# One core, three stages: the first product of the second block by column blocks of its weights over all tokens, with the weights converted there

## Chip, core and metric

The kernel runs on one core of one Trainium2 chip. The metric is the device time of one execution in microseconds (us). Engines: TensorE (PE, matmuls; PEld its weight loads), VectorE (DVE), ScalarE (ACT), GpSimd (POOL), SyncE (SP, which issues most DMAs). Each engine works through its own instructions in their order.

## What is computed

Clustered attention, a mixture of experts, and a dense second block, one after the other, in float64 inputs that carry float32 precision. What matters here:

```python
def _moe_ref(x, w_gate, w_output_gate, w1, w2):        # x: 1536 x 512, 8 experts
    ...
    for e in range(E):
        mask = e_idx == e
        ...
        h = np.maximum(x[mask] @ w1[e], 0.0)           # 512 -> 1024
        ye = h @ w2[e]                                 # 1024 -> 512
        out[mask] = gate_w[mask, None] * eom[mask, e, None] * ye

def _moe2_ref(x, w_in, w_out):                         # 512 -> 2048 -> 512
    h = x @ w_in
    ...
    g = np.where(pos, h, np.where(neg, 0.0, (h + beta) ** 2 / (4.0 * beta)))
    return (g @ w_out).astype(np.float32)
```

## The kernel before

Every matmul operand is held as two float16 halves, high and low, and a product is three matmuls: high x high, high x low, low x high. So each weight has to be split on the chip after its transfer: ScalarE scales and rounds it to the high half, and VectorE (L1012) or GpSimd (L1009, after an extra ScalarE pass L1007) subtracts to get the low half.

**Experts.** The experts run in order of their size, with room for CAPS = 304, 256, 224, 208, 192, 176, 176, 144 tokens. Their weights come in pieces of 512 KB, four for w1 and four for w2 of each expert, through a ring of six buffers (`stg`). Round r has twelve steps: four units of the second product of expert r (`l2`, 24 matmuls each) and eight of the first product of expert r + 1 (`l1`, 12 matmuls each). In each step first the next piece is asked for on SP's queue (w2 of r + 1, then w1 of r + 2), then the unit's matmuls are issued, and then `pipe.step()` issues what earlier steps left behind for it: the split of a piece one step later on ScalarE and one more step later on VectorE or GpSimd, the evacuation of a unit one step later (`hT`, the hidden halves, by ScalarE L1094 and VectorE L1095; `y`, the product times its gate, by VectorE L1111, then its two halves into `x2` by ScalarE L1113 and VectorE L1114). A round ends with a gate matmul (L1074). Units take their PSUM from a ring of seven banks. The tokens of an expert come by a transposing DMA from `xs`, into which the routing has scattered them (L646).

**w_in.** The weights of the second block are 64-bit words. `piece64` loads 512 KB (128 columns of w_in) into a ring of three buffers; one step later VectorE puts the float32 together in three operations (`cw`, L1032 to L1034, in one PSUM bank); one step later ScalarE makes the high half and a float32 copy; one step later GpSimd subtracts (L1041). NWI = (2, 2, 1, 1, 1, 0, 0, 0) blocks stand at the end of the piece list of each round; the other nine follow in the second block.

**Second block.** The 1536 tokens are three groups of 512. `m1(g, fc)` makes one block of 128 hidden columns for one group: 12 matmuls of 512 columns into one of six banks, then two VectorE, two ScalarE and one GpSimd operation (L1242 to L1250). All 16 blocks of group 0 come first, with nine w_in and five w_out conversions between them, then the second product of group 0 with the other eleven w_out blocks, then the first product of groups 1 and 2, then their second products. The engines take a branch (L1190) between the experts and the second block.

Of the kernel before, what the change touches and what calls it, by code (L numbers as in the profile page):

```python
# [140 lines left out]
def build(tc, q, k, v, centroids, w_gate, w_og, w1, w2, w_in, w_out, out):  # L141
# [842 lines left out]

    big = root.enter_context(tc.tile_pool(name="big", bufs=1))
    x2 = big.tile([128, 2, KD, NTK + CMAX], F16, name="x2")
    wih = big.tile([128, KD, F2], F16, name="wih")
    wil = big.tile([128, KD, F2], F16, name="wil")
    st6 = root.enter_context(tc.tile_pool(name="st6", bufs=3))
    cv = root.enter_context(tc.tile_pool(name="cv", bufs=2))  # L990
    mes = ExitStack()
# [22 lines left out]
    def piece(dst_h, dst_l, src, scale):  # L1014

        a, b = dst_h.shape[1], dst_h.shape[2]
        t = stg.tile([128, a, b], F32, tag="st", name="stg")
        n_lo[0] += 1
        nc.sync.dma_start(out=t, in_=src)
        pool = n_lo[0] > 4 and n_lo[0] % 8 in (1, 4, 6)  # L1020
        pipe.add(lag[0], lambda: halves(dst_h, dst_l, t, scale, pool))

    def piece64(dst_h, dst_l, src, scale):

        a, b = dst_h.shape[1], dst_h.shape[2]
# [3 lines left out]
        def words():
            hi, lo = t[:, :, :, 1], t[:, :, :, 0]  # L1030
            c = psc[0].tile([128, a, b], I32, tag="c", name="cw")
            nc.vector.tensor_scalar(out=c, in0=hi, scalar1=5, scalar2=2, op0=ALU.logical_shift_left, op1=ALU.logical_shift_right)  # L1032
            nc.vector.scalar_tensor_tensor(out=c, in0=hi, scalar=-2 ** 30, in1=c, op0=ALU.bitwise_and, op1=ALU.bitwise_or)  # L1033
            nc.vector.scalar_tensor_tensor(out=c, in0=lo, scalar=29, in1=c, op0=ALU.logical_shift_right, op1=ALU.bitwise_or)  # L1034
            f = c.bitcast(F32)

            def split():
                x = cv.tile([128, a, b], F32, tag="cv", name="cv")
                nc.scalar.activation(out=dst_h, in_=f, func=AF.Copy, scale=scale)
                nc.scalar.activation(out=x, in_=f, func=AF.Copy, scale=scale)  # L1040
                pipe.add(1, lambda: nc.gpsimd.tensor_tensor(out=dst_l, in0=x, in1=dst_h, op=ALU.subtract))  # L1041
            pipe.add(1, split)
        pipe.add(1, words)
# [53 lines left out]
    def l2(r, dc):  # L1097
        cap, c0 = CAP[r], C0[r]
        wh, wl = W[r, 2]
        p = ps.tile([128, 512], F32, tag="p", name="yps")  # L1100
        d = slice(dc * 128, (dc + 1) * 128)
        h = HT[r]
        for f in range(KF):
            nc.tensor.matmul(out=p[:, 0:cap], lhsT=wh[:, f, d], rhs=h[:, 0, f, :], start=(f == 0), stop=False)  # L1104
            nc.tensor.matmul(out=p[:, 0:cap], lhsT=wh[:, f, d], rhs=h[:, 1, f, :], start=False, stop=False)  # L1105
            nc.tensor.matmul(out=p[:, 0:cap], lhsT=wl[:, f, d], rhs=h[:, 0, f, :], start=False, stop=(f == KF - 1))  # L1106
        g = G[r]

        def scaled():
            y = yp.tile([128, cap], F32, tag="y", name="y")  # L1110
            nc.vector.tensor_tensor(out=y, in0=p[:, 0:cap], in1=g, op=ALU.mult)  # L1111
            y0, y1 = x2[:, 0, dc, ds(c0, cap)], x2[:, 1, dc, ds(c0, cap)]
            pipe.add(1, lambda: nc.scalar.activation(out=y0, in_=y, func=AF.Copy))  # L1113
            pipe.add(2, lambda: nc.vector.tensor_tensor(out=y1, in0=y, in1=y0, op=ALU.subtract))  # L1114
        pipe.add(1, scaled, True)
# [2 lines left out]
    ACTDVE = [ET.Activation, ET.DVE]  # L1118
    eid = {}

    NWI = (2, 2, 1, 1, 1, 0, 0, 0)

    def expert(r):
        if r < E:
            eid[r] = reg(regs[0:1, 0, r:r + 1], [ET.SP], E - 1)

    wi2 = w_in.bitcast(I32)
    wiq = [lambda f=f: piece64(wih[:, :, f * 128:(f + 1) * 128], wil[:, :, f * 128:(f + 1) * 128],
                               wi2[:, f * 256:(f + 1) * 256].rearrange("(k p) (f z) -> p k f z", p=128, z=2), SWI) for f in range(KF2)]
# [20 lines left out]
    for r in range(E):  # L1150
        expert(r + 2)
        C0[r] = reg(regs[0:1, 2, r:r + 1], ACTDVE, NTK)
        ld_q = (w2_pieces(r + 1, eid[r + 1]) if r + 1 < E else []) + (w1_pieces(r + 2, eid[r + 2]) if r + 2 < E else [])
        ld_q += [wiq.pop(0) for _ in range(NWI[r])]
        a, b = 0, 0
        if r + 1 == E:
            pipe.flush()
            for _ in wnd:
                pass
            nw = nc.values_load(nwin[0:1, 0:1], min_val=0, max_val=NWIN, skip_runtime_bounds_check_because="a count of windows")  # L1160
        if 0 in PAT.get(r, ()):
# [28 lines left out]
    with tc.If(nw > 0):  # L1190
        with tc.For_i(0, nw, 1) as i:
# [12 lines left out]
            for n in range(KD):  # L1204
# [5 lines left out]

    bes = ExitStack()
    wo_p = bes.enter_context(tc.tile_pool(name="wo", bufs=1))
    woh = wo_p.tile([128, KF2, DM], F16, name="woh")
    wol = wo_p.tile([128, KF2, DM], F16, name="wol")
    gp = bes.enter_context(tc.tile_pool(name="gp", bufs=2))
    ep = bes.enter_context(tc.tile_pool(name="ep", bufs=2))
    psc[0] = bes.enter_context(tc.tile_pool(name="psc2", bufs=2, space=PSUM))
    ps2 = bes.enter_context(tc.tile_pool(name="ps2", bufs=6, space=PSUM))
    wo2 = w_out.bitcast(I32)
    woq = [lambda n=n: piece64(woh[:, n:n + 1, :], wol[:, n:n + 1, :],  # L1220
                               wo2[n * 128:(n + 1) * 128, :].rearrange("(k p) (d z) -> p k d z", p=128, z=2), SWO) for n in range(KF2)]
# [64 lines left out]
    for f in range(KF2):
        if woq:
            woq.pop(0)()
        m2_part(0, range(NW), acc, [f])
        pipe.step()  # L1290
    for t in range(NW):
        pipe.add(1 + t // 2, lambda t=t: put(0, t, acc[t]))
    for g in (1, 2):
        for fc in range(KF2):
            m1(g, fc)
            pipe.step()
    for g in (1, 2):
        for t in range(NW):
            p = m2_tile()
# [37 lines left out]
```

## Time and profile before

| | |
|---|---|
| median of 3 runs | 700.89 us (698.8 to 706.71) |
| the profiled execution: time, span | 703.17 us, 701.4 us |
| mean granted TensorE clock | 0.928 of 2.4 GHz |
| attention and routing, to the first expert matmul | 275.25 us |
| first product of expert 0 | 14.60 us |
| rounds 0 to 6 | 24.96, 22.58, 22.34, 17.32, 21.74, 19.81, 14.40 us |
| round 7 and the branch | 8.65 us |
| second block, to the end of the span | 259.75 us |
| busy over the span | PE 605.7, PEld 387.1, DVE 452.4, ACT 388.9, POOL 335.5 us |

Times in the rows are us from the start of the span, durations us unless ns is written. The granted clock is a share of 2.4 GHz; its lower level is 1.2 GHz (0.5). DMA is the mean busy share of the 16 DMA engines. Matmuls overlap, so the distance of their starts is their pace. A waiting instruction is shown with the idle time of its engine and what ended it, as [1.04 <-ACT hT L1094].

### The profile page before, as it was taken

The page shows a single profiled execution, that of the slowest core. Times are in us where ns is not written, and L with a number is a line of the kernel's source. Part 1 is how long each engine was busy: PE and PEld are TensorE (multiplying, and loading weights), DVE is VectorE, ACT ScalarE, POOL GpSimd, SP SyncE. Part 2 cuts the span into 40 slices and gives each one's busy share as a digit, 9 for nine tenths or more (in the row PEclk, how much of TensorE's full clock was granted, in tenths as well). Part 3 has the DMA queues.
Part 4 walks back from the last instruction along what each step waited for, and adds up shares of the span by engine and source line. Part 5 has one row for each costly group of instructions (what it writes and reads, how often), then busy time and mean ns, then how long its engine had stood idle before and what let it go on. Part 6 is the DMA issues. An engine that isn't in the chain of part 4 may idle for free. (4 is left out here: it accounts for less than half of the span.)

```text
span 701.4 us, 14212 instructions
## 1 busy us (share of the span) xinstructions
PE 605.7 (86%) x5574; PEld 387.1 (55%) x5574; DVE 452.4 (64%) x874; ACT 388.9 (55%) x612; POOL 335.5 (48%) x281
## 2 busy tenths in 40 slices
PE   1898679797979753998897999898999999999996
PEld 1365536565656551688797889343444444444442
DVE  6897968898797952687796686599953445500000
ACT  5388558786768911877686785367533444410000
POOL 8368456766476831246465342276634444321101
PEclk9999867798799955999999899999999999999999
DMA  8786998539723429997999994154631000000000
GB/s 212 167 168 148 188 209 214 133 73 159 139 77 84 77 60 271 315 335 159 263 292 204 289 263 142 62 154 143 196 108 60 1 1 0 1 16 30 16 31 30
DMA packets 142171, 96.29 MB, mean 137 GB/s; under 512 B 97168, under 2 KB 127888, under 8 KB 142096
## 3 DMA queue, kind: packets, MB, share of 16 engines
q1 hardware_dynamic: 139744, 88.60, 51.3%
q0 software_dynamic: 2352, 6.70, 2.7%
q8 instruction: 47, 0.77, 0.5%
q14 instruction: 28, 0.23, 0.1%
HBM read 59.84 MB, written 12.29 MB: 103 GB/s over the span
## 5 line engine op out<-in xcount | busy, mean ns | idle before, releaser
L486 POOL TENSOR_TENSOR pl<-p,ph 128x768 f16<-128x768 f32 x64 | 112.8, 1780 | 54.4 <-ACT ph L480 41.2
L445 DVE TENSOR_REDUCE mq<-s 128x1 f32<-128x768 f32 x96 | 90.4, 949 | 23.2 <-PE s L440 23.0
L475 ACT ACTIVATE p<-st 128x768 f32<-128x768 f32 x96 | 75.9, 810 | 38.6 <-PE st L471 35.6
L1250 POOL TENSOR_TENSOR gt<-gx,gt 128x512 f16<-128x512 f32 x48 | 55.4, 1159 | 72.6 <-ACT gt L1249 72.5
L480 ACT ACTIVATE ph<-p 128x768 f16<-128x768 f32 x96 | 77.5, 847 | 0.8
L508 PE MATMUL pv<-vh,pl 128*128 128x65 f16 x576 | 68.7, 203 | 10.1 <-DVE pl L486 10.1
L1235 PE MATMUL mps<-x,wih 128*128 128x512 f16 x192 | 73.5, 383 | 2.9 <-PEq L1190 2.9
L1244 ACT ACTIVATE sq<-cl,c 128x512 f32<-128x512 f32 x48 | 34.6, 721 | 72.7 <-DVE cl L1242 72.7
L1260 PE MATMUL ops<-woh,gt 128*128 128x512 f16 x192 | 72.8, 379 | 1.5 <-DVE gx L1248 1.5
L1237 PE MATMUL mps<-x,wil 128*128 128x512 f16 x192 | 73.5, 383 | 0.0
L1236 PE MATMUL mps<-x,wih 128*128 128x512 f16 x192 | 73.4, 382 | 0.0
L1261 PE MATMUL ops<-wol,gt 128*128 128x512 f16 x192 | 72.8, 379 | 0.5 <-POOL wol L1041 0.4
L1262 PE MATMUL ops<-woh,gt 128*128 128x512 f16 x192 | 72.8, 379 | 0.0
L470 PE MATMUL st<-aT 128*128 128x384 f16 x192 | 68.4, 356 | 4.4 <-DVE mq L445 3.2
L1242 DVE TENSOR_SCALAR cl<-mps 128x512 f32<-128x512 f32 x48 | 33.1, 689 | 59.8 <-PE mps L1237 59.8
L506 PE MATMUL pv<-vh,ph 128*128 128x65 f16 x576 | 69.6, 204 | 0.0
L507 PE MATMUL pv<-vl,ph 128*128 128x64 f16 x576 | 69.2, 202 | 0.0
L471 PE MATMUL st<-q2T,bT 82*128 82x384 f16 x192 | 68.4, 356 | 0.8 <-DMA q2T<-kq 0.8
L1105 PE MATMUL yps<-hT,w2h 128*128 128x176 f16 (+6 forms) x256 | 63.8, 256 | 6.0 <-DVE hT L1095 5.9
L1104 PE MATMUL yps<-hT,w2h 128*128 128x176 f16 (+6 forms) x256 | 63.6, 255 | 5.4 <-ACT hT L1094 4.1
L1088 PE MATMUL hps<-xt,w1h 128*128 128x176 f16 (+6 forms) x256 | 54.4, 265 | 15.4 <-DMA xt<-xs 14.2
L1106 PE MATMUL yps<-hT,w2l 128*128 128x176 f16 (+6 forms) x256 | 63.9, 256 | 0.0
(220 smaller groups left out, 1483.1 us busy)
## 6 DMA issues: line engine op xcount, KB each, us to landing
stg<-in_moe_w_dram SPq DMA_DIRECT2D x64, 512.0 KB, 7.0
stg<-in_moe_w_in_dram SPq DMA_DIRECT2D x16, 512.0 KB, 6.3
stg<-in_moe_w_out_dram SPq DMA_DIRECT2D x16, 512.0 KB, 3.6
xs<-zrow SPq DMA_DIRECT2D x16, 288.0 KB, 4.0
kqf<-in_k_dram SPq DMA_DIRECT2D x16, 192.0 KB, 3.5
kqf<-in_q_dram SPq DMA_DIRECT2D x16, 192.0 KB, 3.2
vf<-in_v_dram SPq DMA_DIRECT2D x16, 192.0 KB, 3.5
xs<-zrow SPq DMA_DIRECT2D x8, 108.0 KB, 2.9
```

Source lines behind the costliest of these rows:

```text
L445: nc.vector.tensor_reduce(out=mq[:, i, t:t + 1], in_=lg_t.pop((i, t))[:, :, 0:HS], axis=AX.XY, op=ALU.max)
L475: nc.scalar.activation(out=p.rearrange("p (e s) -> p e s", e=2), in_=lg_t.pop(("t", i, c))[:, :, 0:HS], func=AF.Exp, scale=SCALE)
L480: nc.scalar.activation(out=ph_t[i, c], in_=p_t[i, c], func=AF.Copy)
L486: eng.tensor_tensor(out=pl_t[i, c], in0=p_t.pop((i, c)), in1=ph_t[i, c], op=ALU.subtract)
L506: nc.tensor.matmul(out=x[:, 0:D + 1], lhsT=ph[:, sl], rhs=a[:, c, 0:D + 1], start=False, stop=False)
L507: nc.tensor.matmul(out=x[:, 0:D], lhsT=ph[:, sl], rhs=b[:, c, :], start=False, stop=False)
L1235: nc.tensor.matmul(out=p, lhsT=wih[:, kk, f], rhs=x2[:, 0, kk, c], start=(kk == 0), stop=False)
L1236: nc.tensor.matmul(out=p, lhsT=wih[:, kk, f], rhs=x2[:, 1, kk, c], start=False, stop=False)
L1237: nc.tensor.matmul(out=p, lhsT=wil[:, kk, f], rhs=x2[:, 0, kk, c], start=False, stop=(kk == KD - 1))
L1260: nc.tensor.matmul(out=p, lhsT=gt[:, 0, f, c], rhs=woh[:, f, :], start=(f == 0), stop=False)
L1261: nc.tensor.matmul(out=p, lhsT=gt[:, 0, f, c], rhs=wol[:, f, :], start=False, stop=False)
L1262: nc.tensor.matmul(out=p, lhsT=gt[:, 1, f, c], rhs=woh[:, f, :], start=False, stop=(f == KF2 - 1))
```

## The change

1. The second block's first product runs over column blocks: for each of the 16 blocks `fc`, the three groups one after the other. w_in is no longer held whole (`wih`, `wil`) but in a ring of four blocks (`wi_p`); the hidden halves of all three groups are held (`gp` has three buffers).
2. `piece64` is parted into `fetch64` (the load) and `words64` (the conversion). One list orders all 32 blocks; each `convert()` takes the oldest loaded block and asks for the next, so three are under way. The rounds of the experts hold no w_in, but for three loads at the end of round 6's list and three conversions in steps 2, 5 and 8 of round 7. In the second block 21 of the 48 steps of the first product convert a block (13 of w_in, 8 of w_out), and the first eight steps of the second product the rest.
3. `y` is no longer a tile in SBUF: the product is scaled in place in its PSUM bank, and both halves are made from there.
4. Of the expert pieces those with a number of 1 or 5 modulo 8 go to GpSimd, before 1, 4 or 6.
5. As `wih` and `wil` are gone, the tiles of the experts lie at other addresses: `stg` at bytes 72,928 to 97,504 of a partition, before 97,504 to 122,080. Tiles of the routing (`gs`, 72,960 to 79,616) lay there before.

```diff
-    wih = big.tile([128, KD, F2], F16, name="wih")
-    wil = big.tile([128, KD, F2], F16, name="wil")
+    wi_p = root.enter_context(tc.tile_pool(name="wi", bufs=4))
...
-        pool = n_lo[0] > 4 and n_lo[0] % 8 in (1, 4, 6)
+        pool = n_lo[0] > 4 and n_lo[0] % 8 in (1, 5)
...
-            y = yp.tile([128, cap], F32, tag="y", name="y")
-            nc.vector.tensor_tensor(out=y, in0=p[:, 0:cap], in1=g, op=ALU.mult)
+            y = p[:, 0:cap]
+            nc.vector.tensor_tensor(out=y, in0=y, in1=g, op=ALU.mult)
...
-    NWI = (2, 2, 1, 1, 1, 0, 0, 0)
...
+    for fc in range(KF2):
+        if fc + 3 < KF2:
+            slots64[fc, 0] = ("i", fc + 3)
+    nwo = 0
+    for fc in range(KF2):
+        for g in range(3):
+            if (g == 1 and fc % 3 == 1) or (g == 0 and (fc, 0) not in slots64):
+                slots64[fc, g] = ("o", nwo)
+                nwo += 1
...
+    def convert():
+        z, f, t = got.pop(0)
+        if z == "i":
+            WI[f] = [wi_p.tile([128, KD, 128], F16, tag=n, name=n) for n in ("wih", "wil")]
+            words64(t, WI[f][0], WI[f][1], SWI)
+        else:
+            words64(t, WO[0][:, f:f + 1, :], WO[1][:, f:f + 1, :], SWO)
+        fetch()
...
-        ld_q += [wiq.pop(0) for _ in range(NWI[r])]
+        if r + 2 == E:
+            ld_q += [fetch, fetch, fetch]
+        if r + 1 == E:
+            ld_q += [lambda: None] * 2 + [convert, lambda: None, lambda: None] * 3
...
-    gp = bes.enter_context(tc.tile_pool(name="gp", bufs=2))
+    gp = bes.enter_context(tc.tile_pool(name="gp", bufs=3))
...
     for fc in range(KF2):
-        m1(0, fc)
-        if wiq:
-            wiq.pop(0)()
-        elif fc >= KF2 - AHEAD:
-            woq.pop(0)()
-        pipe.step()
+        for g in range(3):
+            m1(g, fc)
+            if (fc, g) in slots64:
+                convert()
+            pipe.step()
     acc = [m2_tile() for _ in range(NW)]
     for f in range(KF2):
-        if woq:
-            woq.pop(0)()
+        if got:
+            convert()
...
-    for g in (1, 2):
-        for fc in range(KF2):
-            m1(g, fc)
-            pipe.step()
```

On VectorE, the end of round 3 (`hT` 128x192 is expert 4's hidden half, x_5482 is `x2`), before:

```order
L1095 SCALAR_TENSOR_TENSOR hT<-hps,hT 128x192
L1114 ISA
L1114 TENSOR_TENSOR x_5482<-y,x_5482 128x208
L1012 SCALAR_TENSOR_TENSOR w1l<-stg,w1h 128x4x256
L1111 TENSOR_TENSOR y<-yps,g 128x208
L1032 TENSOR_SCALAR cw<-stg 128x512
L1033 SCALAR_TENSOR_TENSOR cw<-stg,cw 128x512
L1034 SCALAR_TENSOR_TENSOR cw<-stg,cw 128x512
L1095 SCALAR_TENSOR_TENSOR hT<-hps,hT 128x192 x2
```

and with the change:

```order
L1095 SCALAR_TENSOR_TENSOR hT<-hps,hT 128x192
L1114 ISA
L1114 TENSOR_TENSOR x_5482<-yps,x_5482 128x208
L1011 SCALAR_TENSOR_TENSOR w1l<-stg,w1h 128x4x256
L1111 TENSOR_TENSOR yps<-yps,g 128x208
L1011 SCALAR_TENSOR_TENSOR w1l<-stg,w1h 128x4x256
L1095 SCALAR_TENSOR_TENSOR hT<-hps,hT 128x192 x2
```

The three cw operations ahead of the last two hT of the round are gone; the split of the eighth piece, on GpSimd before, stands in their place.

On SP, the first loads of the experts, with the semaphores that each waits for (DMASW are those of GpSimd's transfers, here the scatters into `xs`; DMAHW those of SP's own), before:

```order
L1046 TENSOR_LOAD regs
L1019 ISA
L1019 DMA stg<-in_moe_w_dram 128x4x256 [waits DMAHW2_49,DMAHW3_49,DMAHW1_49,DMAHW4_49,DMAHW0_49,DMAHW5_49,DVE_49,DMAHW6_49,PE_49,DMAHW7_49,Activation_49,Pool_49]
L1019 ISA
L1019 DMA stg<-in_moe_w_dram 128x4x256 [waits DMAHW4_49]
L1046 TENSOR_LOAD regs
L1065 ISA
L1065 DMA_TRANSPOSE xt<-xs 128x4x304 [waits DMASW7_49,DMAHW5_49,DMASW3_49,DVE_49]
```

and with the change (the row of the first load is cut at its end as printed):

```order
L1046 TENSOR_LOAD regs
L1018 ISA
L1018 DMA stg<-in_moe_w_dram 128x4x256 [waits DMASW6_49,DMASW7_49,DMASW5_49,DMAHW0_49,DMASW4_49,DMAHW1_49,DMASW3_49,DMAHW2_49,DMASW2_49,DMAHW3_49,DMASW1_49,DMAHW4_49,DMASW0_49,DMAHW5_49,DVE_49,DMAHW6_49,PE_49,DMAHW7_49,Activation_49,Poo
L1018 ISA
L1018 DMA stg<-in_moe_w_dram 128x4x256
L1046 TENSOR_LOAD regs
L1065 ISA
L1065 DMA_TRANSPOSE xt<-xs 128x4x304
```

The waits for the scatters have moved from the first transposing load to the first weight load, which stands ahead of it.

## Rows read from the trace of the kernel before

**Rows 1.** Windows, rounds 1 to 6, later products: PE, PEld, DVE, ACT, POOL, PEclk, DMA, GB/s.
```profile
314.81:337.39 22.58, 20.48 (x194) 18.58 (x193) 17.15 (x33) 15.32 (x26) 13.20 (x9) 1.00 0.82 203
337.39:359.73 22.34, 19.97 (x194) 18.84 (x194) 19.74 (x40) 16.39 (x28) 13.48 (x9) 0.92 1.06 269
359.73:377.05 17.32, 17.10 (x195) 16.52 (x194) 13.31 (x27) 13.91 (x25) 12.43 (x8) 1.00 0.98 212
377.05:398.79 21.74, 17.82 (x194) 16.81 (x194) 11.93 (x22) 13.60 (x24) 6.73 (x5) 0.92 1.07 253
398.79:418.60 19.81, 17.22 (x194) 16.16 (x194) 15.76 (x26) 17.34 (x32) 9.71 (x5) 0.91 0.98 283
418.60:433.00 14.40, 13.70 (x194) 13.36 (x193) 11.75 (x25) 10.16 (x23) 4.70 (x3) 1.00 0.68 221
...
537.60:622.50 84.90, 84.90 (x395) 38.48 (x394) 38.35 (x60) 36.74 (x60) 35.41 (x31) 1.00 0.02 8
```

**Rows 2.** Waits of PE, 290 to 434 us: in total, times, longest.
```profile
PE yps L1105 <- DVE hT L1095: 5.9, 7, 2.2
PE yps L1104 <- ACT hT L1094: 4.1, 6, 1.0
PE hps L1088 <- DVE hT L1095: 1.2, 2, 0.9
PE yps L1104 <- DVE y L1111: 1.1, 2, 0.7
PE hps L1089 <- POOL w1l L1009: 0.5, 1, 0.5
```

**Rows 3.** Timeline, PE at 294 us; DVE and PE at 381 us: start, duration.
```profile
294.17 0.29 PE L1104 MATMUL yps<-hT,w2h 128*128 128x304 f16 x1 [1.04 <-ACT hT L1094]
...
381.67 0.69 DVE L1032 TENSOR_SCALAR cw<-stg 128x512 int32<-128x512 int32 x1 [2.11 <-DMA stg<-in_moe_w_in_dram]
...
383.73 0.35 DVE L1095 SCALAR_TENSOR_TENSOR hT<-hps,hT 128x192 f16<-128x192 f32 x1
384.13 0.24 PE L1105 MATMUL yps<-hT,w2h 128*128 128x192 f16 x1 [2.17 <-DVE hT L1095]
```

**Rows 4.** Timeline around the first loads of the experts.
```profile
266.46 0.97 POOL L646 DMA_INDIRECT xs<-pay,pos  x1 [0.30 <-issue]
...
267.16 1.02 SPq L1019 DMA_DIRECT2D stg<-in_moe_w_dram  x2
270.67 1.39 SPq L1065 DMA_TRANSPOSE xt<-xs  x1
...
273.33 2.36 DVE L1012 SCALAR_TENSOR_TENSOR w1l<-stg,w1h 128x1024 f16<-128x1024 f32 x2 [6.11 <-DMA stg<-in_moe_w_dram]
...
275.46 0.46 PE L1089 MATMUL hps<-xt,w1l 128*128 128x304 f16 x1
```

**Rows 5.** VectorE groups by line, 290 to 434 us: busy us, mean ns, idle before.
```profile
L1012 DVE SCALAR_TENSOR_TENSOR w2l<-stg,w2h 128x1024 f16<-128x1024 f32 x23 | 32.0, 1393 | 0.3 <-ACT w2h L1011 0.3
...
L1095 DVE SCALAR_TENSOR_TENSOR hT<-hps,hT 128x176 f16<-128x176 f32 x16 | 5.4, 335 | 10.4 <-ACT hT L1094 10.4
...
L1033 DVE SCALAR_TENSOR_TENSOR cw<-stg,cw 128x512 int32<-128x512 int32 x7 | 4.9, 696 | 0.2
...
L1114 DVE TENSOR_TENSOR x<-y,x 128x176 f32 x7 | 3.0, 433 | 0.0
```

**Rows 6.** Waits of PE in the second block, 441 to 701 us.
```profile
PE mps L1235 <- PEq L1190: 2.9, 1, 2.9
PE ops L1260 <- DVE gx L1248: 1.5, 1, 1.5
PE ops L1261 <- POOL wol L1041: 0.4, 1, 0.4
```

**Rows 7.** The chain that ended last: VectorE, two blocks with a conversion each.
```profile
452.59 0.68 DVE cl L1242
...
455.84 0.68 DVE cl L1242
```

More of the change, by code (lines that the diff above doesn't have):

```diff
@@ L1019, in piece, with fetch64 @@
         nc.sync.dma_start(out=t, in_=src)
-        pool = n_lo[0] > 4 and n_lo[0] % 8 in (1, 4, 6)
+        pool = n_lo[0] > 4 and n_lo[0] % 8 in (1, 5)
         pipe.add(lag[0], lambda: halves(dst_h, dst_l, t, scale, pool))
-    def piece64(dst_h, dst_l, src, scale):
-        a, b = dst_h.shape[1], dst_h.shape[2]
+    def fetch64(src, a, b):
         t = st6.tile([128, a, b, 2], I32, tag="st", name="stg")
         nc.sync.dma_start(out=t, in_=src)
[L1029 to L1043, printed above, removed]
@@ new lines, in fetch64, with words64, split @@
+        return t
+    def words64(t, dst_h, dst_l, scale):
+        a, b = dst_h.shape[1], dst_h.shape[2]
+        hi, lo = t[:, :, :, 1], t[:, :, :, 0]
+        c = psc[0].tile([128, a, b], I32, tag="c", name="cw")
+        nc.vector.tensor_scalar(out=c, in0=hi, scalar1=5, scalar2=2, op0=ALU.logical_shift_left, op1=ALU.logical_shift_right)
+        nc.vector.scalar_tensor_tensor(out=c, in0=hi, scalar=-2 ** 30, in1=c, op0=ALU.bitwise_and, op1=ALU.bitwise_or)
+        nc.vector.scalar_tensor_tensor(out=c, in0=lo, scalar=29, in1=c, op0=ALU.logical_shift_right, op1=ALU.bitwise_or)
+        f = c.bitcast(F32)
+        def split():
+            x = cv.tile([128, a, b], F32, tag="cv", name="cv")
+            nc.scalar.activation(out=dst_h, in_=f, func=AF.Copy, scale=scale)
+            nc.scalar.activation(out=x, in_=f, func=AF.Copy, scale=scale)
+            pipe.add(1, lambda: nc.gpsimd.tensor_tensor(out=dst_l, in0=x, in1=dst_h, op=ALU.subtract))
+        pipe.add(1, split)
@@ L1125, in expert, with fetch @@
             eid[r] = reg(regs[0:1, 0, r:r + 1], [ET.SP], E - 1)
-    wi2 = w_in.bitcast(I32)
-    wiq = [lambda f=f: piece64(wih[:, :, f * 128:(f + 1) * 128], wil[:, :, f * 128:(f + 1) * 128],
-                               wi2[:, f * 256:(f + 1) * 256].rearrange("(k p) (f z) -> p k f z", p=128, z=2), SWI) for f in range(KF2)]
+    wi2, wo2 = w_in.bitcast(I32), w_out.bitcast(I32)
+    WI, WO, got, order64 = {}, {}, [], []
+    for f in range(3):
+        order64.append(("i", f))
+    slots64 = {}
+    for fc in range(KF2):
[7 more added lines that the diff above has]
+                nwo += 1
+    order64 += [slots64[k] for k in sorted(slots64)] + [("o", f) for f in range(nwo, KF2)]
+    feed = list(order64)
+    def fetch():
+        if feed:
+            z, f = feed.pop(0)
+            got.append((z, f, fetch64(wi2[:, f * 256:(f + 1) * 256].rearrange("(k p) (f z) -> p k f z", p=128, z=2), KD, 128) if z == "i" else
+                        fetch64(wo2[f * 128:(f + 1) * 128, :].rearrange("(k p) (d z) -> p k d z", p=128, z=2), 1, DM)))
+    def convert():
[6 more added lines that the diff above has]
+        fetch()
     def row(r):
@@ L1212, in build @@
     wo_p = bes.enter_context(tc.tile_pool(name="wo", bufs=1))
-    woh = wo_p.tile([128, KF2, DM], F16, name="woh")
-    wol = wo_p.tile([128, KF2, DM], F16, name="wol")
-    gp = bes.enter_context(tc.tile_pool(name="gp", bufs=2))
+    WO[0] = woh = wo_p.tile([128, KF2, DM], F16, name="woh")
+    WO[1] = wol = wo_p.tile([128, KF2, DM], F16, name="wol")
+    gp = bes.enter_context(tc.tile_pool(name="gp", bufs=3))
     ep = bes.enter_context(tc.tile_pool(name="ep", bufs=2))
@@ L1218, in build @@
     ps2 = bes.enter_context(tc.tile_pool(name="ps2", bufs=6, space=PSUM))
-    wo2 = w_out.bitcast(I32)
-    woq = [lambda n=n: piece64(woh[:, n:n + 1, :], wol[:, n:n + 1, :],
-                               wo2[n * 128:(n + 1) * 128, :].rearrange("(k p) (d z) -> p k d z", p=128, z=2), SWO) for n in range(KF2)]
     c1 = cst.tile([128, 1], F32, name="c1")
@@ L1231, in m1 @@
         p = ps2.tile([128, N], F32, tag="p", name="mps")
-        f = slice(fc * 128, (fc + 1) * 128)
+        wih, wil = WI[fc]
         c = slice(g * N, (g + 1) * N)
         for kk in range(KD):
-            nc.tensor.matmul(out=p, lhsT=wih[:, kk, f], rhs=x2[:, 0, kk, c], start=(kk == 0), stop=False)
-            nc.tensor.matmul(out=p, lhsT=wih[:, kk, f], rhs=x2[:, 1, kk, c], start=False, stop=False)
-            nc.tensor.matmul(out=p, lhsT=wil[:, kk, f], rhs=x2[:, 0, kk, c], start=False, stop=(kk == KD - 1))
+            nc.tensor.matmul(out=p, lhsT=wih[:, kk, :], rhs=x2[:, 0, kk, c], start=(kk == 0), stop=False)
+            nc.tensor.matmul(out=p, lhsT=wih[:, kk, :], rhs=x2[:, 1, kk, c], start=False, stop=False)
+            nc.tensor.matmul(out=p, lhsT=wil[:, kk, :], rhs=x2[:, 0, kk, c], start=False, stop=(kk == KD - 1))
         g0, g1 = GT[g][:, 0, fc, :], GT[g][:, 1, fc, :]
@@ L1276, in build @@
     NW = N // 128
-    AHEAD = 5
     for fc in range(KF2):
-        m1(0, fc)
-        if wiq:
-            wiq.pop(0)()
-        elif fc >= KF2 - AHEAD:
-            woq.pop(0)()
-        pipe.step()
+        for g in range(3):
[3 more added lines that the diff above has]
+            pipe.step()
     acc = [m2_tile() for _ in range(NW)]
     for f in range(KF2):
-        if woq:
-            woq.pop(0)()
+        if got:
+            convert()
         m2_part(0, range(NW), acc, [f])
```

## The prediction

> **What bounds the kernel now.** I read the windows first, cut at the gate matmuls L1074 that end each round of the experts. Rounds 1 to 6 take 118.2 us together (22.58 + 22.34 + 17.32 + 21.74 + 19.81 + 14.40) [rows 1]. The reader should see that these lengths don't follow the arithmetic. A round streams 96 x (cap of r + cap of r+1) columns: 46,080, 41,472, 38,400, 35,328, 33,792 and 30,720. Round 3, the best of them, takes 17.32 / 38,400 = 0.451 ns a column, and the second block's 395 matmuls of 512 columns 84.90 us, 0.420 ns, both at a granted clock of 1.00. Narrow matmuls won't quite reach the second pace; I use the middle, 0.436. The six rounds, 225,792 columns, would need 98.4 us at it, so about 19.8 us of them are not matmul time. The worst rounds (2, 4, 5) also show a granted clock of 0.92, 0.92 and 0.91: a part of each ran at the lower level, 1.2 GHz.
>
> The waits of the matrix engine say where the rest goes: 12.8 us between 290 and 434 us, 11.2 of them for hT, the hidden halves that ScalarE and VectorE make out of PSUM [rows 2]. They come in bursts at the ends of rounds, and the timeline of the burst at 381 us shows why: VectorE stands 2.11 us for a block of w_in to land, then runs the three cw steps, and only then the hT that is behind them in its order; the matmul waits 2.17 us for that hT [rows 3]. The clock falls right after such a burst. The second block is different: after the last expert the matrix engine waits 1.5 + 0.4 us in all for data [rows 6], and its matrix engine is busy for all of the 84.90 us [rows 1]. So what can be won lies in the rounds, and hardly behind them.
>
> **Term 1, w_in leaves the rounds.** Seven blocks (2, 2, 1, 1, 1 in rounds 0 to 4) lose there a transfer of 512 KB, three cw steps (0.696 us each [rows 5], 2.09 the three), two ScalarE copies and a GpSimd subtraction. Three come back as bare transfers in round 6 and are converted in round 7. Of the 12.8 us of rows 2, 1.1 are for y, and 1.04 stand at 294 us, before the first block is asked for [rows 3]; 10.7 us remain. Clock: 22.34 x 0.08 + 21.74 x 0.08 + 19.81 x 0.09 = 5.3 us [rows 1]. So 16.0 us can be laid to w_in. I take 13.5: late expert weights have a share in it too (0.5 us for w1l [rows 2]), and the eighth piece of each round is now split on VectorE (term 3) where the cw steps stood. Bounds: 5.9 us, if only the waits for VectorE's hT go and no clock comes back, and 19.8 us, the whole excess.
>
> **Term 2, the start of the experts.** The buffers of the weights now lie where tiles of the routing lay, and the order shows it: the first weight load waits for the scatters into xs, for which in the kernel before only the transposing loads wait. The last scatter is issued at 266.46 us, the first load at 267.16, the first transposing load at 270.67 [rows 4]. So the first load moves by up to 3.5 us. Its low half is ready at about 274.5 (the first of two splits that take 2.36 us from 273.33) and used at 275.46 by L1089 [rows 4], a slack of 1.0 us: +2.5 us. Bounds: +1.0, if the load lands faster without the scatters beside it and only the transposing load behind two issues (1.02 us) is late; +4.5, if they slow each other by 2 us. Behind the waiting load on SP's queue stand those transposing loads and all further weights, so nothing hides this.
>
> **Term 3, seven subtractions go from GpSimd to VectorE** (of 64 pieces 15 stay on GpSimd, before 22). VectorE gets one more split a round, 1.39 us [rows 5], and loses cw; ScalarE loses one extra pass. In rounds 3 to 5 VectorE was busy 13.31, 11.93 and 15.76 us [rows 1]: mean 13.7, less 2.1 for a cw trio, plus 1.4, is 13.0 us against 15.6 us of matmuls (107,520 columns at 0.436 ns, by three). Covered: 0; if round 5 stays as full as it was, its 15.76 us against 14.7, +1 to +2.
>
> **Term 4, y stays in PSUM.** No instruction is added. VectorE reading PSUM costs no more here than reading SBUF: hT at 176 columns 335 ns out of PSUM, x at 176 columns 433 ns out of SBUF [rows 5]. What it does cost is the bank: it comes free with y's last reader, two units of work later than with its first. With seven banks the matrix engine may lead VectorE by four units instead of six. It already waited 1.1 us twice for y [rows 2]. I take +1.0; bounds 0 and one wait of a unit (14.7 / 12 = 1.23 us) in each of rounds 3 to 6, +4.9.
> The Trainium skill speaks against this edit: "VectorE: DVE Perf Modes" (section on the TRN2 errata) gives VectorE 120 fixed cycles for a PSUM source and 58 for an SBUF one, 65 ns more at its 0.96 GHz. By it 32 reads of y would cost 2.1 us of VectorE, and were all of that on the path, the sum below would be 691.1 and not 689.0. Rows 5 don't show that difference, and I go by the rows.
>
> **Term 5, round 7 and the hand-over.** Three trios of cw, six copies and three subtractions stand now among the last y and x. One trio stands ahead of the last two writes of x2. The matrix engine waits 2.9 us for its branch there in any case [rows 6], and the first product reads the fourth column block of x2 only after nine matmuls. So 0; without that cover +2.0, the trio.
>
> **Term 6, second block.** A block of the first product without a conversion takes VectorE 1.28 us (38.35 us for 60 instructions, two a block) and the matrix engine 2.58 us (12 x 84.90 / 395) [rows 1]. All 48 blocks and 21 conversions are 48 x 1.28 + 21 x 2.09 = 105 us of VectorE in 124 us of matmuls; the densest group, three blocks and two conversions, is 8.0 against 7.7, the next ones 5.9 against 7.7. Before, 16 blocks carried 14 conversions, 3.25 us each [rows 7] against 2.58, and VectorE fell behind until the second product waited 1.9 us. That wait goes, since two more blocks now lie between the last block of group 0 and the second product: -1.9 (bound 0). Transfers run three conversions ahead, 3 x 124 / 21 = 18 us. The tail is the same.
>
> **Sum.** -13.5 + 2.5 + 0 + 1.0 + 0 - 1.9 = -11.9 us. The profiled execution has a span of 701.4 in a time of 703.17 us, 2.3 us above the median of 700.89. So its span goes to 689.5, and against the median I predict **689.0 us**.
>
> **Rivals.**
> - *The transfers go on to set the pace.* For: the shares of 0.98 to 1.07 in rounds 2 to 5, at 256 GB/s over them (time-weighted) [rows 1]. Then a round shrinks by its bytes alone: the five blocks of rounds 1 to 4, 2.62 MB, are 10.2 us; with the other terms -8.6, **692.3 us**. Against: shares of 0.82 in round 1 and 0.68 in round 6.
> - *The whole excess goes*, as every burst fed the next: -19.8 + 2.5 - 1.9 = -19.2, **681.7 us**. For: clock and lateness carry over from round to round. Against: one more split a round on VectorE.
> - *Slower: the banks.* If VectorE lags by four units, 4.9 us, in the narrow rounds, each of the 16 second products of rounds 3 to 6 holds the matrix engine up by a unit, 16 x 1.23 = 20 us: 689.0 - 1.0 + 20 = **708 us**. For: the y waits are waits for a bank, at the old limit of six units. Against: two of them in 144 us, 1.1 us in all, and less work ahead of y in both queues.
> - *It only moves the work*: conversions that hold the second block up as they did the rounds. For this VectorE would need 19 us more there (105 against 124), and I see nothing that gives it; 3 in 100, at about **700 us**.
>
> **How the numbers follow.** Forecast (684 to 694) 0.56, transfers 0.20, whole excess 0.12, banks 0.07, moved only 0.03, a worse start or hand-over 0.02. A change under 1% (7 us) is about what a measurement of this kernel can't tell from none. Faster by over 1%, below 693.9: most of the forecast (0.54), the whole excess and a quarter to a third of the transfers: 0.72. Within 1%: 0.20. Slower: 0.08. The range leaves out the slow rival and the ends of the others: 682 to 697.
>
> **What would show it.** Term 1: no hT wait over 1 us at the ends of rounds 1 to 4, a granted clock near 1.00 in rounds 2, 4 and 5, rounds 1 to 6 in about 105 us. Term 2: the first load at 270 us or later, the first L1089 near 278. Term 4: waits of yps or hps matmuls for the x subtraction L1114; over 5 us of them and the banks decide. Term 6: no wait of ops for gx, VectorE no busier than 0.9 in the first product. Rounds 2 to 5 still at shares of 1 and near 18 us each would be the transfers. Wrong altogether: rounds 1 to 6 above 112 us, or holes among the mps matmuls.

## The result and the profile after

The changed kernel takes 694.68 us in the median of four runs (694.36 to 694.92), the kernel before 699.89 us beside it. The ratio is 0.988, with a 95% interval of 0.983 to 0.993, and 0.985 (0.980 to 0.990) when it ran a second time on another chip: faster by 1.2 to 1.5%. The ratio is taken over undisturbed executions and isn't the quotient of the two medians (0.993): the kernel before ranges from 698.8 to 706.7 us here, and the verdicts below go by ratios. By the ratio the gain is 8 to 11 us. The forecast was 689.0 us with a range of 682 to 697. The profiled execution has a span of 692.6 us against 701.4, that is -8.8 where the sum of the terms said -11.9.

The windows of rounds 1 to 6, cut at the gate matmuls as in [rows 1] (columns: PE, PEld, DVE, ACT, POOL, granted clock, DMA share, GB/s):

```profile
318.62:338.62 20.00, 20.00 (x195) 18.61 (x194) 15.42 (x31) 13.77 (x23) 9.38 (x6) 1.00 1.00 216
338.62:356.68 18.06, 18.06 (x195) 17.77 (x194) 10.51 (x25) 11.76 (x19) 9.70 (x6) 1.00 1.05 239
356.68:375.19 18.51, 16.99 (x195) 16.60 (x194) 14.94 (x30) 14.04 (x25) 9.58 (x6) 1.00 1.04 238
375.19:390.68 15.49, 15.49 (x195) 15.24 (x194) 11.93 (x20) 11.84 (x21) 5.36 (x3) 1.00 1.05 291
390.68:407.59 16.91, 15.06 (x195) 14.71 (x194) 14.40 (x26) 14.54 (x28) 4.28 (x2) 1.00 1.08 306
407.59:421.62 14.03, 13.71 (x194) 13.36 (x193) 10.90 (x25) 8.28 (x20) 2.13 (x1) 1.00 0.56 185
```

Together 103.0 us, before 118.2. The granted clock is 1.00 in all six, and in rounds 1, 2 and 4 the matrix engine doesn't stand at all. But the DMA share is 1.00 to 1.08 in five of them. The waits of the matrix engine between 289 and 422 us, beside the 12.8 us of [rows 2]:

```profile
PE yps L1104 <- DVE hT L1095: 2.6, 3, 1.2
PE yps L1106 <- DVE w2l L1011: 1.2, 2, 0.7
PE hps L1088 <- DVE hT L1095: 1.1, 2, 0.8
PE yps L1104 <- ACT hT L1094: 0.9, 1, 0.9
PE yps L1105 <- DVE hT L1095: 0.2, 1, 0.2
```

6.0 us are left, none of them for a reader of `y`. So the rounds went about as forecast; one wait for `hT` of 1.2 us remains, where the prediction wanted none over 1 us. The two ends of the stage did not go as forecast. Its beginning (timeline: start, duration; beside [rows 4]), and round 0:

```profile
265.04 0.97 POOL L646 DMA_INDIRECT xs<-pay,pos  x1 [0.30 <-issue]
...
269.38 1.02 SPq L1018 DMA_DIRECT2D stg<-in_moe_w_dram  x2
270.86 1.77 SPq L1065 DMA_TRANSPOSE xt<-xs  x1
272.78 2.03 SPq L1066 DMA_TRANSPOSE xt<-xs  x1
...
276.54 0.41 PE L1088 MATMUL hps<-xt,w1h 128*128 128x304 f16 x1 [16.93 <-DMA xt<-xs]
```

```profile
290.73:318.62 27.89, 25.56 (x195) 19.27 (x194) 21.39 (x30) 21.85 (x32) 7.38 (x4) 0.94 0.96 302
```

From the last scatter to the first matmul it is 11.50 us, before 275.25 - 266.46 = 8.79. Round 0 takes 27.89 us, before 24.96. And the hand-over to the second block, GpSimd (the low half of block 0), VectorE, ScalarE and matrix engine:

```profile
427.06 1.16 POOL L1042 TENSOR_TENSOR wil<-cv,wih 128x512 f16<-128x512 f32 x1 [13.50 <-ACT cv L1041]
...
428.44 0.68 DVE L1033 TENSOR_SCALAR cw<-stg 128x512 int32<-128x512 int32 x1
...
430.49 0.51 DVE L1114 TENSOR_TENSOR x<-yps,x 128x144 f32 x2
...
431.73 0.69 DVE L1033 TENSOR_SCALAR cw<-stg 128x512 int32<-128x512 int32 x1 [0.73 <-ACT cv L1041]
...
433.92 0.60 ACT L1040 ACTIVATE wih<-cw 128x512 f16<-128x512 f32 x1 [2.22 <-DVE cw L1035]
434.41 0.59 ACT L1041 ACTIVATE cv<-cw 128x512 f32<-128x512 f32 x1
...
435.10 0.58 PE L1263 MATMUL mps<-x,wih 128*128 128x512 f16 x1 [7.14 <-ACTq L1221]
```

The first matmul of the second block waits 7.14 us, before 2.9 [rows 6], and starts just when ScalarE has made the copy of the third w_in block. Behind it the matrix engine waits for nothing any more (PE's waits from 421 us to the end are this one row):

```profile
PE mps L1263 <- ACTq L1221: 7.1, 1, 7.1
```

The whole difference, from one profiled execution to the other: routing -1.4 (the last scatter is issued at 265.04 instead of 266.46, which the change doesn't touch), start of the experts +2.7, first product of expert 0 -0.4, round 0 +2.9, rounds 1 to 6 -15.2, hand-over +4.2, second block -1.6 (257.5 from its first matmul to the end, before 701.4 - 442.26 = 259.1). That is -8.8.

### The profile page after: what moved, and what is told of

Its sections match the earlier page's. It is cut to its first block, busy times and chain, and to the rows that moved or that the text cites. A ratio compares the mean times of both kernels' runs of the same rounds, so it can differ in the third digit from the quotient of the medians.

```text
span 692.6 us, 14218 instructions
## 1 busy us (share of the span) xinstructions
PE 599.5 (87%) x5574; PEld 383.0 (55%) x5574; DVE 453.3 (65%) x881; ACT 380.5 (55%) x605; POOL 322.6 (47%) x274
## 5 line engine op out<-in xcount | busy, mean ns | idle before, releaser
L1088 PE MATMUL hps<-xt,w1h 128*128 128x176 f16 (+6 forms) x256 | 51.7, 257 | 18.1 <-DMA xt<-xs 16.9
L440 PE MATMUL s<-bT 80*128 80x384 f16 x192 | 52.5, 372 | 13.8 <-DMA bT<-kq 7.1
```

## The experiments

Theory: w_in in the rounds cost what rounds 1 to 6 gave back, mostly through VectorE; the late start comes from the memory of the weight buffers; the long hand-over from three conversions ahead of the branch. Rivals: the transfers alone set the pace; the gain is that of the other edits; the branch itself takes the time. All lengths are from one profiled execution each, cut at the gate matmuls; "start" is from the issue of the last scatter to the first expert matmul, "hand-over" the wait of the first matmul of the second block. Ratios are to the kernel before on the same chip.

| kernel | start | round 0 | rounds 1 to 6 | hand-over | median us | ratio (95%) |
|---|---|---|---|---|---|---|
| before | 8.8 | 25.0 | 118.2 | 2.9 | 699.89 | 1 |
| before, second profile | 9.4 | 27.5 | 124.8 | 3.4 | 704.53 | |
| changed | 11.5 | 27.9 | 103.0 | 7.1 | 694.68 | 0.988 (0.983 to 0.993) |
| changed, second time | 12.3 | 27.6 | 108.4 | 7.1 | 695.57 | 0.985 (0.980 to 0.990) |
| w_in loaded and converted again | 12.1 | 24.5 | 120.1 | 7.1 | 709.43 | 1.008 (1.004 to 1.013) |
| only loaded again | 11.6 | 27.4 | 113.4 | 7.1 | 703.09 | 0.999 (0.995 to 1.004) |
| only converted again | 11.4 | 27.2 | 116.7 | 7.1 | 709.80 | 1.012 (1.006 to 1.018) |
| 22 pieces on GpSimd | 11.4 | 27.5 | 109.4 | 7.1 | 698.01 | 0.990 (0.985 to 0.995) |
| one conversion ahead of the branch | 11.9 | 30.0 | 110.2 | 4.3 | 693.51 | 0.983 (0.979 to 0.988) |
| weight buffers moved | 9.6 | 25.1 | 105.4 | 7.1 | 693.33 | 0.983 (0.978 to 0.988) |
| both of these | 10.1 | 24.8 | 108.2 | 3.7 | 688.28 | 0.978 (0.973 to 0.982) |
| y in SBUF | 11.6 | 27.2 | 104.1 | 7.1 | 695.42 | 0.978 (0.972 to 0.985) |
| both, y in SBUF | 10.0 | 27.5 | 106.7 | 3.6 | 689.79 | 0.977 (0.972 to 0.981) |
| both, y in SBUF, 22 pieces on GpSimd | 9.6 | 24.6 | 110.2 | 3.9 | 692.61 | 0.983 (0.978 to 0.987) |

### w_in back in the rounds: whole, as transfers, as conversions

```diff
+    NWI = (2, 2, 1, 1, 1, 0, 0, 0)
+    more = iter(range(8))
+    def again():
+        f = next(more)
+        t = fetch64(wi2[:, f * 256:(f + 1) * 256]..., KD, 128)
+        pipe.add(1, lambda: words64(t, scr[0], scr[1], SWI))
...
+        ld_q += [again] * NWI[r]
```

The second kernel has the load without `words64`, the third `words64` on a block that is loaded once.

> The changed kernel with seven extra w_in blocks loaded and converted again at the end of rounds 0 to 4 (2, 2, 1, 1, 1, as before); their results go into a spare tile that nobody reads. If w_in in the rounds is what cost the 15.2 us that rounds 1 to 6 got shorter by (118.2 to 103.0): rounds 1 to 6 come back to 112 to 118 us, waits for hT of over 1 us at the ends of rounds 1 to 4 and granted clocks under 0.95 after them, time 704 to 711 us. If the gain came from the other edits (the eighth piece on VectorE, y in PSUM): rounds 1 to 6 stay under 106 us, time under 698 us.

Measured: rounds 1 to 6 in 120.1 us and 709.43 us. The rounds are again as long as before, with the pattern of the eighth piece and `y` in PSUM left as changed. So the move of w_in is what shortened them.

> The changed kernel with the seven extra w_in blocks loaded at the same places, but not converted (their data is read by nobody). If the transfers set the pace of the rounds: five blocks of 512 KB in rounds 1 to 4 at 256 GB/s are 10 us, rounds 1 to 6 at 112 us or more, time 704 us or more. If the work on VectorE is what holds the matmuls up: rounds 1 to 6 at most 3 us above the 103.0 of the changed kernel, time 694 to 698 us.

Measured: 113.4 us and 703.09 us, where the theory of VectorE alone wanted 106 and at most 698. The longest wait, and ScalarE ahead of it:

```profile
380.63 1.06 ACT L1010 ACTIVATE w1h<-stg 128x1024 f16<-128x1024 f32 x1 [3.16 <-DMA stg<-in_moe_w_dram]
381.59 0.33 ACT L1113 ACTIVATE x<-yps 128x208 f32 x1
381.82 0.32 ACT L1094 ACTIVATE hT<-hps 128x192 f16<-128x192 f32 x1
...
382.58 0.31 PE L1088 MATMUL hps<-xt,w1h 128*128 128x176 f16 x1 [4.43 <-DVE hT L1095]
```

ScalarE stands 3.16 us for an expert weight that has not landed; `hT` is behind it in its order, and the matmul waits 4.43 us. So a late transfer arrives at the matrix engine under the name of `hT`. That the bytes of w_in make the expert weights later is read from the time, 0.999 against 0.985 to 0.988 for the changed kernel; a single wait of this kind also occurs without them, as the second profile of the changed kernel shows below.

> The changed kernel with the seven extra conversions at the same places, all from one block that is loaded once in round 0: three VectorE, two ScalarE and one GpSimd operation each, no transfers beyond the one. If the work on VectorE ahead of hT is the cause: rounds 1 to 6 at 108 to 115 us, time 700 to 707 us. If it is the transfers (or VectorE standing at a block that has not landed): at most 3 us above 103.0, time 694 to 698 us.

Measured: 116.7 us and 709.80 us, above the band of the theory. VectorE, ScalarE and the matrix engine at one of the waits:

```profile
343.55 0.68 DVE L1036 TENSOR_SCALAR cw<-still 128x512 int32<-128x512 int32 x1
344.26 0.70 DVE L1037 SCALAR_TENSOR_TENSOR cw<-still,cw 128x512 int32<-128x512 int32 x1
345.00 0.70 DVE L1038 SCALAR_TENSOR_TENSOR cw<-still,cw 128x512 int32<-128x512 int32 x1
...
345.78 0.60 ACT L1043 ACTIVATE scrh<-cw 128x512 f16<-128x512 f32 x1 [1.73 <-DVE cw L1038]
346.28 0.59 ACT L1044 ACTIVATE cv<-cw 128x512 f32<-128x512 f32 x1
346.76 0.36 ACT L1097 ACTIVATE hT<-hps 128x224 f16<-128x224 f32 x1
...
346.97 0.38 DVE L1098 SCALAR_TENSOR_TENSOR hT<-hps,hT 128x224 f16<-128x224 f32 x1
...
347.41 0.34 PE L1107 MATMUL yps<-hT,w2h 128*128 128x224 f16 x1 [3.46 <-DVE hT L1098]
```

Here nothing waits for a transfer: ScalarE stands 1.73 us for the conversion, its two copies go first, then its `hT`, then VectorE's. So a conversion delays `hT` on two engines one after the other. The changed kernel's rounds ran five times in these studies (the two of the kernel itself, and the three with only the hand-over or the buffers changed): 103.0, 108.4, 110.2, 105.4 and 108.2, mean 107.0. Beside that mean the transfers alone cost 6.4 us, the conversions alone 9.7, both 13.1. These are single profiles beside a spread of 7 us, so the sizes are rough. The ratios agree on the order: 0.999 with the transfers, 1.012 with the conversions, 1.008 with both, against 0.985 to 0.988. Each costs something by itself, and the conversions more. How far the two add is not shown.

### Seven pieces back to GpSimd

```diff
-        pool = n_lo[0] > 4 and n_lo[0] % 8 in (1, 5)
+        pool = n_lo[0] > 4 and n_lo[0] % 8 in (1, 4, 6)
```

> The changed kernel with 22 instead of 15 pieces on GpSimd (numbers 1, 4 or 6 modulo 8, as before). By the prediction's third term, a cost of nothing for the seven splits on VectorE: time 693 to 697 us, rounds 1 to 6 within 2 us of 103.0. If the seven splits that went to VectorE are what makes the bursts at 360 and 394 us (1.2 and 1.1 us of waits for hT): these go, time 690 to 692. If fewer GpSimd pieces are part of the gain: rounds 1 to 6 at 106 us or more, time 698 us or more.

Measured: 698.01 us, ratio 0.990, rounds 1 to 6 in 109.4. The bursts didn't go, they lie elsewhere (3.6 us at 377 us, 1.9 at 341). By its numbers this is the third band, but it is inconclusive: the interval overlaps with those of both runs of the changed kernel, and the changed kernel itself took 108.4 us over these rounds in its second profile.

### One conversion ahead of the branch

```diff
-            ld_q += [lambda: None] * 2 + [convert, lambda: None, lambda: None] * 3
+            ld_q += [lambda: None] * 2 + [convert]
...
-    for f in range(3):
-        order64.append(("i", f))
+    order64.append(("i", 0))
...
-    for fc in range(KF2):
+    slots64[0, 0], slots64[0, 1], slots64[0, 2] = ("i", 1), ("i", 2), ("i", 3)
+    for fc in range(1, KF2):
```

> The changed kernel with one conversion in round 7 instead of three; blocks 1 and 2 are converted after the first two steps of the second block, block 3 after the third. In the changed kernel the first matmul of the second block waits 7.1 us, until ScalarE has copied the third block (before: 2.9 us), and then runs at the lower clock until 440.5 us. If this first matmul waits for everything that VectorE and ScalarE have ahead of the branch: its wait falls to 2.5 to 3.5 us, the stretch at the lower clock gets shorter, time 4 to 6 us below that of the changed kernel (694.7), 688 to 691 us. If it only waits for its own block 0 and the branch itself takes the time: the wait stays near 7 us, time 694 to 696 us. If the second block can't take three conversions in its first three steps: waits of mps matmuls for wih or wil, 692 us or more.

Measured: the wait falls to 4.3 us, less far than the 2.5 to 3.5 expected, and the second block waits for no weight:

```profile
437.70 0.82 DVE L1114 TENSOR_TENSOR x<-yps,x 128x144 f32 x3
...
441.74 0.58 PE L1263 MATMUL mps<-x,wih 128*128 128x512 f16 x1 [4.30 <-DVE cw L1033]
```

So 2.8 of the 7.1 us were those of the two further conversions. With three of them the first matmul starts 0.10 us behind the end of ScalarE's last copy (434.41 + 0.59 = 435.00, then 435.10), though the weights of its own block 0 had been ready since 428.22 and the last write of x2 since 431.00. With one conversion it starts 3.2 us behind VectorE's last operation ahead of the branch (437.70 + 0.82 = 438.52), so what is left of the wait is not that of work ahead of the branch. The cw operation that the row names is the first of block 1, behind the branch (441.04 to 441.73); with both edits, below, the row names the branch itself (L1221). In time the edit alone stays open: a median of 693.51 us, above the 688 to 691 expected. The profiled execution, with a round 0 of 30.0 us, took 700.91 us.

### The weight buffers behind the routing's tiles

```diff
+    xp_ = mes.enter_context(tc.tile_pool(name="xp", bufs=2))
     stg = mes.enter_context(tc.tile_pool(name="stg", bufs=6))
...
-    xp_ = mes.enter_context(tc.tile_pool(name="xp", bufs=2))
```

> The changed kernel with the buffers of the weights 10,944 bytes further on (the tokens' tiles lie in front of them now), so that they lie behind the tiles of the routing that the scatters read. If the memory is the cause of the late start: the first weight load about 3 us after the last scatter is issued no longer, but about 0.7 us; the first expert matmul 2 to 3 us earlier, measured from the last scatter; round 0 back from 27.9 to about 25 us, as its weights come earlier; time 4 to 6 us below the changed kernel's 694.7, 689 to 691 us. If round 0 is longer for another reason: only the start, 691.5 to 693 us. If the transposing loads set the start: within 1 us of 694.7.

Measured: 693.33 us; the profiled execution takes 692.58 us with a start of 9.6 us and a round 0 of 25.1.

```profile
265.61 0.97 POOL L646 DMA_INDIRECT xs<-pay,pos  x1 [0.30 <-issue]
266.20 1.02 SPq L1018 DMA_DIRECT2D stg<-in_moe_w_dram  x2
270.34 1.38 SPq L1065 DMA_TRANSPOSE xt<-xs  x1
...
275.21 0.41 PE L1088 MATMUL hps<-xt,w1h 128*128 128x304 f16 x1 [15.01 <-DVE w1l L1011]
```

The load follows the last scatter after 0.59 us, not 4.34, and the transposing load still comes 4.7 us behind it. The first matmul comes 1.9 us earlier, a little less than the 2 to 3 expected. So the addresses made most of the late start. The time lies just above the middle band (691.5 to 693), start without round 0, and says nothing sure on round 0.

### Both edits, and what is left of the change

> The changed kernel with both edits, one conversion ahead of the branch and the weight buffers behind the routing's tiles. If the two costs are independent and both real: the sum of the two gains, 682 to 687 us. If the late start is taken up by something later, or the wait at the second block comes back as another: 688 us or more.

Measured: 688.28 us, ratio 0.978 (0.973 to 0.982), a start of 10.1 us and this hand-over:

```profile
PE mps L1263 <- PEq L1221: 3.7, 1, 3.7
```

It lies just inside the second band: 6.4 us below the changed kernel by the medians, where two gains of 4 to 6 us were hoped for. It is faster than the kernel before. Beside the changed kernel its interval lies below that of the first run and overlaps with that of the second.

> The changed kernel with y as a tile in SBUF again, its PSUM bank free after the first of its readers. By the prediction's fourth term (+1.0 for the bank, bounds 0 to 4.9): 690 to 694.7 us, likeliest 693.7. By the rival of the banks most of rounds 3 to 6 would get shorter by over 5 us together: below 690. If y in PSUM costs nothing: 694 to 695.5 us. The VectorE page of the Trainium skill on DVE perf modes gives a PSUM source 62 cycles more than an SBUF one, 65 ns; 32 reads of y out of SBUF would by that be 2.1 us less of VectorE, of which the time would show at most that.

Measured: a median of 695.42 us, by which `y` in PSUM costs nothing, but a ratio of 0.978 (0.972 to 0.985). The six executions range from 685.38 to 698.27 us, and the ratio rests on the three shortest. By itself it would speak for `y` in SBUF, so it was tried once more on top of the two edits:

```diff
-            y = p[:, 0:cap]
-            nc.vector.tensor_tensor(out=y, in0=y, in1=g, op=ALU.mult)
+            y = yp.tile([128, cap], F32, tag="y", name="y")
+            nc.vector.tensor_tensor(out=y, in0=p[:, 0:cap], in1=g, op=ALU.mult)
```

> The changed kernel with one conversion ahead of the branch, the weight buffers behind the routing's tiles, and y in SBUF again. If the bank that y holds costs what the two fast executions of the variant with y in SBUF suggest (2 to 4 us): 684 to 687 us. If y in PSUM costs nothing: 687.5 to 690 us, as with the two edits alone (688.3).

Measured: 689.79 us, ratio 0.977 against 0.978 with `y` in PSUM. The bank that `y` holds costs nothing that can be measured. This kernel ran on one chip with the changed one: all six of its executions (686.24 to 690.67 us) lie below all six of that (692.73 to 701.12). With `y` measuring the same in either place, the two repairs together shorten the changed kernel.

> The same as the kernel ahead of it, and the pieces 1, 4 and 6 modulo 8 on GpSimd as before: so of the whole change only the move of w_in is left, with one conversion ahead of the branch and the early start. If the move of w_in alone is the gain: within 2 us of the kernel ahead of it. If the seven splits on VectorE are part of the gain (GpSimd's late halves hold the matmuls up): 3 us or more above it. If they cost: 2 us or more below it.

Measured: 692.61 us, ratio 0.983 (0.978 to 0.987): 2.8 us above the kernel ahead of it, with rounds 1 to 6 of 110.2 us. It leans to the second band, as the same edit did above (0.990), but the intervals still overlap. Of the ratios to before, the move of w_in with the two repairs alone gives 0.983.

### The two kernels profiled a second time

> The changed kernel as it is, a second time, beside the variants on one chip, to see how far one profiled execution of it differs from another. The four kernels so far that share its rounds spread from 103.0 to 110.2 us over rounds 1 to 6. If its rounds always run alike: rounds 1 to 6 within 2 us of 103.0. If it depends on when each weight lands: anywhere from 103 to 110, with waits for hT behind a ScalarE split that stands at its load. Its wait at the second block 7.1 us in either case. Time 692 to 698 us.

Rounds 1 to 6 took 108.4 us this time, 5.4 more than in the first profile, of the same program. The biggest difference is one hole of 4.0 us:

```profile
361.41 1.06 ACT L1010 ACTIVATE w1h<-stg 128x1024 f16<-128x1024 f32 x1 [2.85 <-DMA stg<-in_moe_w_dram]
362.37 0.33 ACT L1094 ACTIVATE hT<-hps 128x208 f16<-128x208 f32 x1
...
362.73 0.37 DVE L1095 SCALAR_TENSOR_TENSOR hT<-hps,hT 128x208 f16<-128x208 f32 x1 [5.14 <-ACT hT L1094]
...
363.15 0.24 PE L1074 MATMUL gp<-xt,ones 2*128 2x208 f16 x1 [4.00 <-DVE hT L1095]
```

It is the chain of the second experiment, without any w_in in the rounds: what differs here is when an expert weight lands.

> The kernel before, profiled a second time. If its excess in rounds 1 to 6 is regular: 115 to 121 us there, waits for hT at the ends of rounds 0 to 4 behind the w_in conversions. If the 118.2 us were a bad execution: under 112 us, and the gain of the changed kernel in the rounds is overstated.

124.8 us, above the band, at granted clocks of 0.87 and 0.86 in rounds 2 and 4:

```profile
332.16:358.25 26.09, 21.52 (x194) 19.65 (x194) 22.98 (x43) 18.66 (x31) 14.26 (x10) 0.87 1.05 263
...
376.99:401.32 24.33, 18.95 (x195) 17.60 (x194) 11.96 (x22) 14.80 (x25) 7.09 (x6) 0.86 0.99 231
```

The excess of before was no accident of one execution. By means it is 121.5 against 107.0: 14.5 us.

## Why the prediction was right in direction and short on one step

**Term 1** (w_in leaves the rounds, -13.5) was right in size: -15.2 between the two first profiles, -14.5 by means, against -12.5 for terms 1, 3 and 4 together. The clock came back as said. There is some luck in the first number: 103.0 us is the shortest of the five profiles of these rounds. Its picture was too narrow: it laid the waits to VectorE's conversions, and a part came through the transfers, by way of ScalarE (6.4 beside 9.7 us in the two experiments). The rival of the transfers was half right: the shares of 1.00 to 1.08 in rounds 1 to 5 are the sign that the prediction named for it, and rounds 2 and 3 are near its 18 us (18.06 and 18.51), though in round 2 the matrix engine was busy all the time. Late transfers may also make the spread from 103 to 110 us; this is shown for one hole of 4.0 us only.

**Term 2** (start, +2.5) measured +2.7, mostly for the reason given. The first load came 0.6 us earlier than the bound named (269.38, in a run whose scatters were 1.4 us earlier), and the wait that ended last was that for the transposing load, not for the low half (in five of the eight profiles with the overlap it was the low half). Over these eight the start is 11.4 to 12.3 us, over the four of the changed kernel without the overlap 9.6 to 10.1, over the two of before 8.8 and 9.4. So by means the addresses make 1.9 of 2.6 us; the rest stays open. What the term left out is round 0: its weights come late too, the matrix engine waits 0.66 and 0.57 us for low halves of w2 and 0.88 for `hT` between 292 and 297 us, and part of what follows runs at the lower level, 1.2 GHz:

```profile
295.00:300.00 5.00, 3.78 (x16) 2.12 (x17) 3.31 (x5) 4.77 (x7) 2.12 (x1) 0.71 1.08 343
```

That was +2.9 us. That the late start made it is argued, not shown: with an early start round 0 took 24.6 to 25.1 us three times and 27.5 once, with a late one 27.2 to 30.0 seven times and 24.5 once, and the second profile of before has 27.5 too.

**Term 3** (splits to VectorE, 0): the sign may be the other way. Both kernels with 22 pieces on GpSimd had a higher ratio than their partners, by 0.002 to 0.006; the intervals overlap, so it stays open.

**Term 4** (y in PSUM, +1.0): no wait for a reader of `y` appeared, and the pair of kernels differs by 0.1%. The rival of the banks is out.

**Term 5** (hand-over, 0) is the step that failed. It said that the 2.9 us for the branch cover one trio ahead of the last two writes of x2, and bounded the loss at 2.0. It looked only at the operands of the first product. But the first matmul behind the branch waited for what ScalarE had ahead of the branch, the third conversion with its two copies included, 4.1 us after the last write of x2 (431.00 to 435.10). What in the program makes it wait is not shown here; that the two further conversions made the wait is shown, as it fell to 4.3 and 3.7 us without them. And the three run in a chain: `cw` has one PSUM bank there, so the trio of a block waits until ScalarE has copied the one before ([0.73 <-ACT cv L1041] above), 3.3 us from one to the next (428.44 to 431.73), while round 7 holds 6.3 us of matmuls. Measured +4.2. Behind the wait the granted clock over the next 5.4 us was 0.50 and 0.69 in the two profiles of the changed kernel, 0.68 and 1.00 in those of before: by these means about 1.3 us more, which stand in the second block's sum.

**Term 6** (second block, -1.9) measured -1.6, and -1.1 between the second profiles (257.6 to 256.5): the waits for gx and wol are gone, and VectorE is busy 0.82 of the first product:

```profile
445.00:560.00 115.00, 115.00 (x535) 52.16 (x533) 94.71 (x149) 73.45 (x129) 72.85 (x64) 1.00 0.30 92
```

In sum the terms were 3.1 us short in span. That it is not more is partly luck: -1.4 came from the routing, which the change doesn't touch, and rounds 1 to 6 gave 2.7 more than terms 1, 3 and 4. Against that stand +4.2 from the hand-over and +2.9 from round 0, for which the prediction had no term. The rest of the 5.7 us between 689.0 and 694.68 is the place of the two executions: that of before was 2.3 us above the median it was set against, that of after is 0.3 below its own.

## What to carry to other kernels

When work is moved to the far side of a branch or a loop, count what the first instruction there waits for: here it waited for the last work that an engine had ahead of the branch, and not only for its operands. A smaller or moved buffer shifts all that is allocated after it; look at what the new addresses make the first load wait for. And a wait in the name of one engine may have its cause two engines back: follow the chain to the one that stands at a transfer before laying it to the work in between.

## What the runs showed of the hardware

The subtraction of x L1114, between 290 and 435 us: before with `y` in SBUF, and in the changed kernel with `y` in PSUM (busy us, mean ns):

```profile
L1114 DVE TENSOR_TENSOR x<-y,x 128x304 f32 x4 | 4.5, 1113 | 0.9 <-ACT x L1113 0.7 <-DVE hT L1095 0.2
```

```profile
L1114 DVE TENSOR_TENSOR x<-yps,x 128x304 f32 x4 | 1.8, 461 | 0.0
```

Two of the four of before, with GpSimd's work beside them:

```profile
301.11 2.25 POOL L1009 TENSOR_TENSOR w2l<-stg,w2h 128x1024 f16<-128x1024 f32 x1 [0.81 <-ACT w2h L1008]
...
302.31 1.38 DVE L1114 TENSOR_TENSOR x<-y,x 128x304 f32 x1 [0.21 <-DVE hT L1095]
...
304.00 0.46 DVE L1114 TENSOR_TENSOR x<-y,x 128x304 f32 x1
```

And one of the four with the change, beside the same kind of work:

```profile
310.59 2.13 POOL L1008 TENSOR_TENSOR w1l<-stg,w1h 128x1024 f16<-128x1024 f32 x1 [6.92 <-ACT w1h L1007]
...
311.25 0.47 DVE L1114 TENSOR_TENSOR x<-yps,x 128x304 f32 x1
```

Alone the operation takes 0.46 us from either memory, so the 65 ns more for PSUM that the prediction quoted do not show. With both inputs in SBUF it took 1.38 us while a GpSimd subtraction ran, and it ended 0.33 us behind that. Of the 28 subtractions of before in this window six ran beside one of GpSimd's; these six took 0.92 to 2.16 us and ended 0.20 to 0.33 us behind it. With `y` in PSUM the five that ran beside one took 0.33 to 0.47 us. In term 4 the prediction set VectorE's 433 ns for x from SBUF [rows 5] against 335 ns for `hT` from PSUM without seeing that the 433 held such a block: six of the seven took 324 to 331 ns, one 1066. The 1.39 us of a split in term 3 hold them too: alone a split takes 1.21 us. The Trainium skill, "SBUF — State Buffer" (section on the two separate sides), says that a VectorE operation with two SBUF inputs and a GpSimd operation that reads SBUF take turns at a shared pair of ports, whole instructions long; the rows agree. So `y` in PSUM takes an operation out of GpSimd's way. In time this could not be measured (0.978 against 0.977).
